# A feed-forward stage without GpSimd: leaky ReLU as one ScalarE activation, low parts on VectorE

## The chip, the cores and the metric

The kernel runs on one core of one Trainium2 chip. The metric is the device time of one execution in microseconds, the median of several runs. TensorE multiplies matrices (weights are loaded by a separate step, PEld), VectorE and ScalarE work elementwise here on SBUF and PSUM, GpSimd elementwise on SBUF, and SyncE (SP) issues the DMAs.

## The reference

A block of three parts. The first is a linear attention with a complex decay over batch 4, 8 heads, 768 positions and head size 48. The second is a soft mixture of 8 experts with 4 slots each. The third, the one that the change touches, is a feed-forward on 3072 tokens of width 384 with a hidden width of 2048:

```
h = x @ w_in                  # [3072, 384] @ [384, 2048]
g = np.maximum(0.01 * h, h)   # leaky ReLU, slope 0.01
return g @ w_out              # [3072, 2048] @ [2048, 384]
```

`x` is the output of the mixture, `c @ slot_out`, with `c` the softmax of the logits over 32 slots. Its rank is therefore 32, and the kernel multiplies `slot_out @ w_in` first (`product`), which leaves an inner dimension of 32 for `h`.

## The kernel before

**Number format.** Matmuls of the feed-forward take fp32r operands. To keep accuracy a value is split in two: the high part is the value written as fp32r, the low part is the value minus the high part, also written as fp32r. An output tile adds three products: high by high, low by high, high by low.

**Tiling.** The 3072 tokens form 8 groups (j = 0 to 7) of 384 tokens, and the hidden width forms 16 blocks (f) of 128. For one pair (j, f) `ffn1` (lines 1004 to 1016) has one matmul of 128x384 into a PSUM bank (line 1007). Line 1009 (ScalarE) copies 0.01 times the bank to an SBUF tile `x`, line 1010 (VectorE) takes the maximum of this tile and the bank, line 1011 (ScalarE) writes the high part into a tile of tag `w`, and the low part is made by GpSimd for j = 1 (line 1013) and by VectorE for all other j (line 1015). `ffn2` (lines 1020 to 1038) then has three matmuls for each of the three token tiles of j (lines 1028 to 1030); a bank for each tile adds up over all 16 f. After the last f line 1037 copies the bank out and line 1038 stores it.

**Output weights.** `w_out` arrives as 64-bit words, one block of 384 columns for each f. `conv_wo` loads a block into one of two `raw` buffers, and `narrow` (lines 417 to 424) makes fp32 of it in five steps: line 420 on ScalarE, lines 421, 422, 423 and 424 on VectorE, through one of two `tmp` buffers. Then GpSimd writes the high part (line 452) and the low part (line 453). `conv_wi` uses the same `narrow` for the input weights, much earlier and without the split.

**Loops.** Groups j = 0 and 1 run together, f by f: for each f a conversion four blocks ahead, two `ffn1` two blocks ahead and six `ffn2` steps, 20 matmuls in all. This needs six output banks, and leaves two of the eight for `ffn1`. Groups j = 2 to 7 follow one by one, when all weights are split.

**Order.** Nothing is issued in source order. Every operation is put into a planner with its engine, an estimated cost (`c_dve`, `c_act`, `c_ptt`, `c_pts`), its operands and its results; the planner goes backward from the end to give each a latest time, and forward to write an order for each engine. Every engine then works through its own list in order. Costs of moved operations thus enter the order of the whole program. The activation tables of ScalarE are loaded where the planner says (line 251).

Of the kernel before, what the change touches and what calls it, by code (L numbers as in the profile page):

```python
# [10 lines left out]
F32 = mybir.dt.float32  # L11
F32R = mybir.dt.float32r
I32 = mybir.dt.int32
AF = mybir.ActivationFunctionType
ALU = mybir.AluOpType
# [15 lines left out]
NG = 3 * P  # L31
# [240 lines left out]
def c_dve(n):  # L272
    return 0.069 + 1.04e-3 * n
# [6 lines left out]
def c_act(n):  # L280
    return 0.095 + 0.83e-3 * n


def c_ptt(n):
    return 0.15 + 2.11e-3 * n


def c_pts(n):
    return 0.1 + 0.92e-3 * n
# [3 lines left out]
def tile_kernel(  # L293
# [14 lines left out]
    V, A, GP, T, SY = nc.vector, nc.scalar, nc.gpsimd, nc.tensor, nc.sync  # L308
# [3 lines left out]
    def pe(cost, fn, r=(), w=(), **k):  # L312
        return plan.add("PE", cost, fn, r, w, **k)

    def act(n, fn, r=(), w=(), **k):
        return plan.add("ACT", c_act(n), fn, r, w, **k)

    def dve(cost, fn, r=(), w=(), **k):
        return plan.add("DVE", cost, fn, r, w, **k)

    def pool(cost, fn, r=(), w=(), **k):
        return plan.add("POOL", cost, fn, r, w, **k)
# [29 lines left out]
    HW = W // 2  # L352
# [75 lines left out]
    def conv(src, i, dst):  # L428

        raw = t_raw()  # L430
        load(raw, None, src[:, 2 * HW * i:2 * HW * (i + 1)].rearrange("p (n w) -> p n w", w=2), P * HW * 8)
        tmp = t_tmp()
        d, dk = dst(tmp)
        narrow(
            HW, d, dk, raw, lambda: raw()[:, :, 0], lambda: raw()[:, :, 1],
            (tmp, 0), (tmp, 1), lambda: tmp()[:, 0], lambda: tmp()[:, 1],
        )
        return tmp
# [7 lines left out]
    def conv_wo(i):  # L446
        j, h = divmod(i, 2)
        if h == 0:
            woh[j], wol[j] = t_w([P, 2, HW], F32R), t_w([P, 2, HW], F32R)
        tmp = conv(wo_in, i, lambda tmp: (lambda: tmp()[:, 1], (tmp, 1)))  # L450
        wh, wl = woh[j], wol[j]
        pool(c_pts(HW), lambda: GP.tensor_scalar(wh()[:, h], tmp()[:, 1], 1.0, 0.0, op0=ALU.mult, op1=ALU.add), [(tmp, 1)], [(wh, h)])
        pool(c_ptt(HW), lambda: GP.tensor_tensor(wl()[:, h], tmp()[:, 1], wh()[:, h].bitcast(F32), op=ALU.subtract), [(tmp, 1), (wh, h)], [(wl, h)])


    st = [dict() for _ in range(NU)]
# [547 lines left out]
    def ffn1(j, f):  # L1004
        b = bank()
        w, o = gs[f // 4], P * (f % 4)
        pe(0.17, lambda: T.matmul(b()[:, :NG], lhsT=w()[:, o:o + P], rhs=cT[j](), start=True, stop=True), [(w, o // 256), cT[j]], [b])  # L1007
        u, g = t_x(), t_w([P, 2, NG], F32R)
        act(NG, lambda: A.activation(u(), b()[:, :NG], AF.Copy, scale=0.01), [b], [u])  # L1009
        dve(c_dve(NG), lambda: V.tensor_tensor(u(), u(), b()[:, :NG], op=ALU.max), [b], [u])  # L1010
        act(NG, lambda: A.activation(g()[:, 0], u(), AF.Copy), [u], [(g, 0)])  # L1011
        if j == 1:
            pool(c_ptt(NG), lambda: GP.tensor_tensor(g()[:, 1], u(), g()[:, 0].bitcast(F32), op=ALU.subtract), [u, (g, 0)], [(g, 1)])
        else:
            dve(c_dve(NG), lambda: V.tensor_tensor(g()[:, 1], u(), g()[:, 0].bitcast(F32), op=ALU.subtract), [u, (g, 0)], [(g, 1)])  # L1015
        hl[j, f] = g

    ob = {}
# [38 lines left out]
    for f in FO[:4]:  # L1057
        conv_wo(f)
    for f in FO[:ahead]:
        for j in range(2):  # L1060
            ffn1(j, f)
    for i, f in enumerate(FO):
        if i < NFC - 4:
            conv_wo(FO[i + 4])
        for j in range(2):
            if i + ahead < NFC:
                ffn1(j, FO[i + ahead])
        for j in range(2):
            for t in range(3):
                ffn2(j, t, f)  # L1070
    for j in range(2, NB):
        if j == 3:
            combine_t(6, NB, bank, ("cw", 6))
        for f in FO:
            ffn1(j, f)
            if j < NB - 1:
                for t in range(3):
                    ffn2(j, t, f)
# [54 lines left out]
```

## Time and profile before

| | |
|---|---|
| median of 3 runs | 546.22 us (546.16 to 546.89) |
| profiled execution | 546.49 us, span 544.8 us |
| mean granted TensorE clock | 0.997 |
| busy: TensorE matmul | 492.4 us (90%) |
| busy: VectorE | 401.4 us (74%) |
| busy: ScalarE | 367.0 us (67%) |
| busy: GpSimd | 56.9 us (10%), 75 instructions |

The busy shares are means over stages that differ. The page divides the span into 40 slices of 13.6 us, and the stage of the feed-forward begins in slice 23, counted from 1. A group of the profile is all instructions of one line, engine and shape; "idle before" is the time that the engine stood still just before them, with what ended it. In a timeline consecutive instructions of one group can be merged (x2, x3).

### The profile page before, as it was taken

The page shows a single profiled execution, that of the slowest core. Times are in us where ns is not written, and L with a number is a line of the kernel's source. Part 1 is how long each engine was busy: PE and PEld are TensorE (multiplying, and loading weights), DVE is VectorE, ACT ScalarE, POOL GpSimd, SP SyncE. Part 2 cuts the span into 40 slices and gives each one's busy share as a digit, 9 for nine tenths or more (in the row PEclk, how much of TensorE's full clock was granted, in tenths as well). Part 3 has the DMA queues.
Part 4 walks back from the last instruction along what each step waited for, and adds up shares of the span by engine and source line. Part 5 has one row for each costly group of instructions (what it writes and reads, how often), then busy time and mean ns, then how long its engine had stood idle before and what let it go on. Part 6 is the DMA issues. An engine that isn't in the chain of part 4 may idle for free.

```text
span 544.8 us, 10467 instructions
## 1 busy us (share of the span) xinstructions
PE 492.4 (90%) x3985; PEld 432.5 (79%) x3985; DVE 401.4 (74%) x796; ACT 367.0 (67%) x693; POOL 56.9 (10%) x75
## 2 busy tenths in 40 slices
PE   2488979999999999997898877779999999999997
PEld 1277768888889888885544766779999999999997
DVE  2577898998999999897525999986548643986510
ACT  7879999799999986945103644547457545976612
POOL 1000000000000000001002566660000000000000
PEclk9999999999999999999899999999999999999999
DMA  7953254442353586878794233311010002000002
GB/s 273 393 155 109 42 147 143 131 143 80 88 170 78 168 265 225 292 259 255 254 403 135 60 87 88 87 31 43 1 58 16 2 1 73 29 1 2 29 1 101
DMA packets 43846, 66.98 MB, mean 123 GB/s; under 512 B 19098, under 2 KB 24970, under 8 KB 43796
## 3 DMA queue, kind: packets, MB, share of 16 engines
q1 hardware_dynamic: 43476, 66.29, 37.5%
q8 instruction: 31, 0.51, 0.4%
q0 software_dynamic: 320, 0.03, 0.1%
q14 instruction: 19, 0.16, 0.1%
HBM read 61.53 MB, written 4.75 MB: 122 GB/s over the span
## 4 chain that ended last, share of the span: by engine, by line
PE 60%; DVE 18%; ACT 11%; DMA 7%; issue 3%; SPq 0%; ACTq 0%; DVEq 0%
PE b L1029 10%; PE b L1030 10%; PE b L1028 10%; PE btr L622 6%; PE bm L662 5%; PE bsc L637 5%; PE bm L680 4%; PE bc L545 4%; PE b L1007 3%; DMA w<-in_w_dram 3%; DVE tmp L421 3%; ACT L251 2%; DVE tmp L423 2%; DVE tmp L422 2%; DVE x L1010 2%
## 5 line engine op out<-in xcount | busy, mean ns | idle before, releaser
L1028 PE MATMUL b<-w 128*128 128x384 f32 x384 | 129.0, 336 | 0.7 <-ACT w L1011 0.6
L1029 PE MATMUL b<-w 128*128 128x384 f32 x384 | 129.0, 336 | 0.5 <-DVE w L1015 0.5
L1030 PE MATMUL b<-w 128*128 128x384 f32 x384 | 128.5, 335 | 0.0
L1010 DVE TENSOR_TENSOR x<-x,b 128x384 f32<-128x384 f32 x128 | 68.9, 550 | 40.1 <-ACT x L1009 38.6
L1011 ACT ACTIVATE w<-x 128x384 fp32r<-128x384 f32 x128 | 65.6, 525 | 43.9 <-DVE x L1010 39.2
L1015 DVE TENSOR_TENSOR w<-x,w 128x384 fp32r<-128x384 f32 x112 | 62.0, 566 | 15.7 <-PE b L1007 8.9
L1028 PEld LDWEIGHTS b<-w 128*128 128x128 f32 x384 | 72.1, 188 | 1.6 <-issue 0.9
L1029 PEld LDWEIGHTS b<-w 128*128 128x128 f32 x384 | 72.1, 188 | 1.0 <-DVE w L1015 1.0
L1009 ACT ACTIVATE x<-b 128x384 f32<-128x384 f32 x128 | 60.3, 487 | 18.6 <-PE b L1007 8.6
L1030 PEld LDWEIGHTS b<-w 128*128 128x128 f32 x384 | 72.1, 188 | 0.0
L637 PE MATMUL bsc<-qt,kt 96*128 96x128 f32 x384 | 51.7, 280 | 0.1
L637 PEld LDWEIGHTS bsc<-qt,kt 96*128 96x128 f32 x384 | 46.6, 193 | 2.6 <-issue 1.5
L640 DVE TENSOR_TENSOR sc<-bsc,tri_r 128x512 f32<-128x512 f32 x48 | 32.8, 685 | 12.8 <-PE bsc L637 9.1
L1037 ACT ACTIVATE k<-b 128x384 f32<-128x384 f32 x24 | 11.8, 492 | 43.2 <-PE b L1030 42.8
L662 PE MATMUL bm<-sc,w 128*64 128x128 f32 (+1 forms) x384 | 37.7, 282 | 2.0 <-ACT x L711 1.3
L1007 PE MATMUL b<-q,qt 128*128 128x384 f32 x80 | 26.5, 356 | 13.5 <-DVE x L1010 13.4
L622 PE MATMUL btr<-ident,q 128*96 128x128 f32 x192 | 30.6, 283 | 5.4 <-DVE q L607 5.0
L251 ACT ACT_TABLE_LOAD x27 | 34.6, 1283 | 1.2 <-PEq L1122 0.8
L680 PEld LDWEIGHTS bm<-w,k 128*96 128x96 f32 x320 | 31.7, 170 | 4.6 <-ACT x L711 2.3
L680 PE MATMUL bm<-w,k 128*96 128x48 f32 x320 | 33.6, 252 | 1.9 <-ACT x L711 1.9
L628 ACT ACTIVATE qt<-btr 96x512 f32<-96x512 f32 x48 | 28.0, 589 | 7.0 <-PE btr L622 4.5
L662 PE MATMUL bm<-qt,S 96*48 96x128 f32 x320 | 31.2, 272 | 0.0
(175 smaller groups left out, 862.3 us busy)
## 6 DMA issues: line engine op xcount, KB each, us to landing
w<-in_w_dram SPq DMA_DIRECT2D x49, 384.0 KB, 5.7
w<-in_qkv_dram SPq DMA_DIRECT2D x36, 384.0 KB, 4.2
w<-in_a_dram SPq DMA_DIRECT2D x22, 384.0 KB, 4.6
raw<-in_wi_dram SPq DMA_DIRECT2D x16, 384.0 KB, 3.5
raw<-in_wo_dram SPq DMA_DIRECT2D x16, 384.0 KB, 3.2
out_dram<-k SPq DMA_DIRECT2D x24, 192.0 KB, 1.9
cs<-in_w_dram SPq DMA_DIRECT2D x6, 384.0 KB, 5.8
k<-in_w_dram SPq DMA_DIRECT2D x6, 192.0 KB, 5.1
```

What stands on the lines that cost most here:

```text
L251: self.preload(TABLES[o.table])
L622: T.transpose(b()[:96, P * i:P * i + P], src()[:, i].rearrange("p t d -> p (t d)"), ident)
L637: T.matmul(b()[:, P * i:P * i + P], lhsT=k()[:96, i, :], rhs=q()[:96, i, :], start=True, stop=True)
L662: T.matmul(y()[64 * j:64 * j + m, o:o + P], lhsT=l, rhs=r, start=kind == 0, stop=kind == 1 or c == 0)
L680: T.matmul(b()[:96, o:o + n], lhsT=k()[:, i].rearrange("p t d -> p (t d)"), rhs=v()[:, D * g:D * g + n], start=True, stop=True)
L1009: act(NG, lambda: A.activation(u(), b()[:, :NG], AF.Copy, scale=0.01), [b], [u])
L1010: dve(c_dve(NG), lambda: V.tensor_tensor(u(), u(), b()[:, :NG], op=ALU.max), [b], [u])
L1011: act(NG, lambda: A.activation(g()[:, 0], u(), AF.Copy), [u], [(g, 0)])
L1015: dve(c_dve(NG), lambda: V.tensor_tensor(g()[:, 1], u(), g()[:, 0].bitcast(F32), op=ALU.subtract), [u, (g, 0)], [(g, 1)])
L1028: T.matmul(b()[:, :DM], lhsT=lh, rhs=wh()[:, i], start=f == FO[0], stop=False)
L1029: T.matmul(b()[:, :DM], lhsT=ll, rhs=wh()[:, i], start=False, stop=False)
L1030: T.matmul(b()[:, :DM], lhsT=lh, rhs=wl()[:, i], start=False, stop=f == FO[-1])
```

## The change

Two functions change. In `conv_wo` the high part of the output weights is written by ScalarE and the low part by VectorE. In `ffn1` one ScalarE activation, Prelu with alpha 0.01, takes the place of the scaled copy and the maximum, and the low part is on VectorE for every j. GpSimd keeps a copy in `combine_t` (line 853).

```diff
@@ conv_wo
-        pool(c_pts(HW), lambda: GP.tensor_scalar(wh()[:, h], tmp()[:, 1], 1.0, 0.0, op0=ALU.mult, op1=ALU.add), [(tmp, 1)], [(wh, h)])
-        pool(c_ptt(HW), lambda: GP.tensor_tensor(wl()[:, h], tmp()[:, 1], wh()[:, h].bitcast(F32), op=ALU.subtract), [(tmp, 1), (wh, h)], [(wl, h)])
+        act(HW, lambda: A.activation(wh()[:, h], tmp()[:, 1], AF.Copy), [(tmp, 1)], [(wh, h)])
+        dve(c_dve(HW), lambda: V.tensor_tensor(wl()[:, h], tmp()[:, 1], wh()[:, h].bitcast(F32), op=ALU.subtract), [(tmp, 1), (wh, h)], [(wl, h)])
@@ ffn1
-        act(NG, lambda: A.activation(u(), b()[:, :NG], AF.Copy, scale=0.01), [b], [u])
-        dve(c_dve(NG), lambda: V.tensor_tensor(u(), u(), b()[:, :NG], op=ALU.max), [b], [u])
+        act(NG, lambda: A.activation(u(), b()[:, :NG], AF.Prelu, alpha=0.01), [b], [u])
         act(NG, lambda: A.activation(g()[:, 0], u(), AF.Copy), [u], [(g, 0)])
-        if j == 1:
-            pool(c_ptt(NG), lambda: GP.tensor_tensor(g()[:, 1], u(), g()[:, 0].bitcast(F32), op=ALU.subtract), [u, (g, 0)], [(g, 1)])
-        else:
-            dve(c_dve(NG), lambda: V.tensor_tensor(g()[:, 1], u(), g()[:, 0].bitcast(F32), op=ALU.subtract), [u, (g, 0)], [(g, 1)])
+        dve(c_dve(NG), lambda: V.tensor_tensor(g()[:, 1], u(), g()[:, 0].bitcast(F32), op=ALU.subtract), [u, (g, 0)], [(g, 1)])
```

## Rows read from the trace of the kernel before

**Rows 1.** The page: busy tenths of 40 equal slices of the span.
```profile
PE   2488979999999999997898877779999999999997
...
DVE  2577898998999999897525999986548643986510
...
POOL 1000000000000000001002566660000000000000
```

**Rows 2.** Windows: length, then per engine busy us (instructions); clock, DMA.
```profile
299.92:365.45 65.53, 51.43 (x268) 45.87 (x269) 64.84 (x104) 34.42 (x76) 39.49 (x42) 1.00 0.26 73
386.00:413.50 27.50, 27.50 (x161) 27.46 (x161) 14.06 (x29) 15.80 (x37) 0.00 (x0) 1.00 0.10 37
```

**Rows 3.** Timeline of TensorE: start us, length us, engine, line, [idle before].
```profile
341.00 0.44 PE L1007 MATMUL b<-q,qt 128*128 128x384 f32 x1 [1.49 <-DVE x L1010]
...
345.78 0.44 PE L1007 MATMUL b<-q,qt 128*128 128x384 f32 x1 [1.02 <-DVE x L1010]
...
533.52 0.33 PE L1029 MATMUL b<-w 128*128 128x384 f32 x1
...
536.64 0.33 PE L1029 MATMUL b<-w 128*128 128x384 f32 x1
```

**Rows 4.** Timeline of VectorE, 340 to 346 us.
```profile
341.33 0.55 DVE L1010 TENSOR_TENSOR x<-x,b 128x384 f32<-128x384 f32 x1
341.80 0.68 DVE L1015 TENSOR_TENSOR w<-x,w 128x384 fp32r<-128x384 f32 x1
342.41 1.17 DVE L421 TENSOR_SCALAR tmp<-tmp 128x384 f32<-128x384 f32 x1
343.61 1.05 DVE L422 TENSOR_SCALAR tmp<-tmp 128x384 int32<-128x384 int32 x1
344.69 0.56 DVE L423 SCALAR_TENSOR_TENSOR tmp<-raw,tmp 128x384 int32<-128x384 int32 x1
345.17 0.55 DVE L1010 TENSOR_TENSOR x<-x,b 128x384 f32<-128x384 f32 x1
```

**Rows 5.** Groups, VectorE, 325 to 361 us: busy us, mean ns | idle before.
```profile
L421 DVE TENSOR_SCALAR tmp<-tmp 128x384 f32<-128x384 f32 x7 | 8.2, 1169 | 0.0
```

**Rows 6.** Groups, 20 to 280 us, three engines.
```profile
L421 DVE TENSOR_SCALAR tmp<-tmp 128x384 f32<-128x384 f32 x16 | 5.5, 354 | 2.4 <-ACT tmp L420 2.3
...
L853 POOL TENSOR_SCALAR kt<-logits 128x192 fp32r<-128x192 f32 x8 | 3.2, 404 | 71.1 <-PE bsc L637 38.1 <-PE b L920 24.0 <-DVE sc L640 4.9
...
L569 ACT ACTIVATE cs<-cs,b_hpi 128x384 f32<-128x384 f32 x1 | 0.6, 603 | 0.0
```

**Rows 7.** One line's instructions: the table loads, min/median/max ns.
```profile
L251 ACT ACT_TABLE_LOAD  x27: 1283/1283/1283, 0.8 to 226.0; - x27
```

**Rows 8.** Timeline, 290 to 300 us, the start of the stage.
```profile
290.92 0.36 DVE L421 TENSOR_SCALAR tmp<-tmp 128x384 f32<-128x384 f32 x1 [4.65 <-ACT tmp L420]
...
291.32 0.36 DVE L422 TENSOR_SCALAR tmp<-tmp 128x384 int32<-128x384 int32 x1
...
293.93 1.26 DVE L423 SCALAR_TENSOR_TENSOR tmp<-raw,tmp 128x384 int32<-128x384 int32 x1
...
299.92 0.41 PE L1028 MATMUL b<-w 128*128 128x384 f32 x1 [0.60 <-ACT w L1011]
```

**Rows 9.** Timeline of ScalarE, 340 to 346 us.
```profile
340.98 0.53 ACT L1011 ACTIVATE w<-x 128x384 fp32r<-128x384 f32 x1 [2.44 <-DVE x L1010]
341.41 0.54 ACT L420 ACTIVATE tmp<-raw 128x384 f32<-128x384 f32 x1
341.92 0.53 ACT L1011 ACTIVATE w<-x 128x384 fp32r<-128x384 f32 x1
342.35 0.92 ACT L1009 ACTIVATE x<-b 128x384 f32<-128x384 f32 x2
```

**Rows 10.** Tile raw, 290 to 372 us: issue to landing of its loads.
```profile
DMA to landing us min/median/max: 3.0/3.2/3.4
```

**Rows 11.** Groups, 290 to 365 us: the weight copies on GpSimd.
```profile
L452 POOL TENSOR_SCALAR w<-tmp 128x384 fp32r<-128x384 f32 x15 | 7.8, 518 | 36.8 <-DVE tmp L424 27.0 <-PE b L1007 9.8
```

## The prediction

> **What bounds the kernel now.** I read the page first. Its slices tell two stages of the feed-forward apart: in slices 23 to 27 (counted from 1) VectorE stands at 8 or 9, TensorE at 7 or 8 and GpSimd at 5 or 6; from slice 28 on TensorE stands at 9 and GpSimd at 0 [rows 1]. Then I cut the stage with the windows view, from the first output matmul (299.92) to the place where the chain of waits goes over to TensorE (365.45). There VectorE is busy 64.84 of 65.53 us, GpSimd 39.49, ScalarE only 34.42, and TensorE shows 268 matmuls; afterwards TensorE is busy all of the time (27.50 of 27.50) and VectorE half of it; the granted clock is 1.00 in both, the higher of its two levels, 2.4 GHz [rows 2]. In the later stretch matmuls of this shape start 0.1733 us apart: 18 of them between 533.52 and 536.64 [rows 3]. So the 268 needed 46.4 us, and TensorE lost 65.5 - 46.4 = 19.1 us in the first stretch. Everything behind it is a full TensorE, so a microsecond won there reaches the end whole. That loss is the most that the stage can give back.
>
> The period shows who makes it. The first of the two matmuls of line 1007 starts at 341.00 and, one f later, at 345.78, and each time it waited for the maximum of line 1010 on VectorE, which holds its PSUM bank [rows 3]. One step of f costs 4.78 us in which TensorE has 2 + 18 = 20 matmuls, 20 x 0.1733 = 3.47 us. The timeline of VectorE shows where 4.78 comes from: seven instructions, and two of them, the scalar operations of lines 421 and 422, take 1.17 and 1.05 us, while GpSimd computes [rows 4]. Over 325 to 361 us line 421 averages 1169 ns [rows 5]. The same line, same shape, converts the input weights between 20 and 280 us, where GpSimd does little (eight copies of 404 ns), and takes 354 ns, 16 times over [rows 6]; line 422 does the same. The two lose some 0.8 and 0.7 us to their neighbour.
>
> **The change part by part.** *Counts.* For one f (both j of 0 and 1), VectorE loses two maxima (line 1010) and gains the low part of j = 1 and the low part of the weights: seven instructions before and seven after. Moved work alone wins nothing there; the gain must come from what each instruction costs once GpSimd is silent. GpSimd keeps only the copy of line 853, eight of them, all before 280 us [rows 6], so the stage has none left.
>
> *VectorE after.* The two scalar operations fall to 0.36 us, and since each waits for the one ahead of it, some 0.40 apart (290.92 to 291.32 when the first weights are converted [rows 8]). The other five start 0.47 us apart where nothing holds them: 345.17 - 344.69 = 0.48, 341.80 - 341.33 = 0.47 [rows 4]. Sum: 0.40 + 0.40 + 5 x 0.47 = 3.15 us. The low part of the weights has no row on VectorE; its nearest rows are lines 1015 and 1010 of the same shape, at 0.47 apart (0.55 of record) and, beside GpSimd, 0.61 apart (0.68) [rows 4]. I take 0.47, since no GpSimd is beside it; 0.61 would make the sum 3.3.
>
> The Trainium skill, "VectorE: DVE Perf Modes", section "The DRAIN you can't avoid", says that the pipe is flushed behind each operation and that the next one waits, though one that is not held starts earlier. The trace bears the exception: starts 0.47 us apart under records of 0.55. Without the exception the sum would be that of the records, 2 x 0.36 + 5 x 0.55 = 3.47, a tie with TensorE.
>
> *ScalarE after.* For one f it has the two copies of line 1009, two of line 1011 and line 420 now; the first two become Prelu, and one weight copy is added. Starts lie 0.43 apart (340.98 to 341.41) and 0.51 behind line 420 (341.41 to 341.92) [rows 9]: 5 x 0.43 + 0.51 = 2.66 us. No row shows a Prelu. Nearest below is line 1009 itself, the copy that it takes the place of (0.49 each: 0.92 for two), nearest above an activation with a bias tensor at 603 ns [rows 6, 9]. I take 0.49, the same operands and shape. At 603 the sum is 2.9, still under 3.47, so both ends give one answer; below a copy nothing suggests it could go.
>
> The Trainium skill, "ScalarE: Activation LUTs", section "Table sets: the hidden batching unit", lists relu, copy, identity and abs as members of every set and does not name a parametric one. By it one load might be due before the first Prelu; a load takes 1283 ns here [rows 7], so the sum would be at most 1.3 us longer.
>
> *GpSimd.* Its 16 weight copies, 16 weight low parts and 16 low parts of j = 1 go. They were not on the path themselves.
>
> *What is late next.* TensorE with 3.47 against 3.15 and 2.66. Two things keep it from running without a gap. First, VectorE is at 91% with queues in order; an instruction that waits for its operand holds those behind it. Second, the loads of the output weights have two buffers: a buffer is free again after line 424, the load lands 3.2 us later [rows 10], then come line 420 (0.54) and 0.40 + 0.40 + 0.48 + 0.47 + 0.55 of VectorE, 6.04 us for two, 3.02 per f. That fits under 3.47 by 0.45. Issue of the loads on SP stays as it is. Line 453's place is taken by VectorE and frees the temporary earlier or at the same time. The bank of line 1007 is now free after one ScalarE activation and no longer after VectorE's maximum, which takes away the very wait that set the period.
>
> For these gaps I charge 2.5 us over the 16 f: little in steady state, most in the first 10 us, where VectorE has the last of the small product and three conversions at once. Bounds: 0 (everything hidden), and 7, if each of 16 f loses 0.45 more (3.9 in place of 3.47).
>
> *Start of the stage.* The first output matmul waits for line 1011 [rows 8], which waits for the maximum [rows 9]. A maximum (0.55) falls out of that chain. Earlier, line 423 took 1.26 us at 293.93 beside GpSimd, 0.7 over its later record of 0.56 [rows 4, 8]; against it stand the weight low parts, 0.47 each, now in VectorE's queue at that time. I take 0.6 us, between 0 and 1.4.
>
> *Later groups, j of 2 and above.* VectorE loses 16 maxima in each and ScalarE keeps its two activations; TensorE is full there already [rows 2], so nothing changes.
>
> **Sum:** -19.1 - 0.6 + 2.5 = -17.2 us. The profiled execution took 546.49 us (1.7 around its span of 544.8); its forecast is 529.3. The median of the runs shown is 546.22, 0.27 less, and the forecast for it is 529.0. Bounds of the terms: 546.2 - 19.1 - 1.4 = 525.7, and 546.2 - 19.1 + 7 = 534.1.
>
> **Rivals.**
> *The weight conversion is late.* VectorE in order and two load buffers make the conversions the bound. For it: 6.04 us for two loads holds only if ScalarE takes line 420 at once and VectorE nothing else in between; with three activations ahead of it (1.3) and two foreign VectorE instructions (0.94) it is 8.3, 4.15 per f. Counted from the third conversion at some 301 us (an estimate from the start of the stage), the 16th ends at 301 + 13 x 4.15 = 355, 3.7 us after TensorE would want it (299.3 + 15 x 3.47 = 351.4), beside the gaps of the forecast: 529.0 + 3.7 = 533, up to 537 with the start as it was. Against it: four conversions run ahead, and TensorE has slack to give.
>
> *Lines 421 and 422 stay slow.* Then VectorE needs 1.20 + 1.08 + 5 x 0.47 = 4.63 in place of 4.78, some 0.1 over about ten f: 545. Against it: 354 ns wherever GpSimd is idle [rows 6].
>
> *ScalarE is held by the weight copy (slower).* GpSimd stood idle 36.8 us ahead of 15 copies of line 452, mostly for line 424 [rows 11]; that was free. On ScalarE the same wait at the head of the queue holds the Prelus behind it, and so the banks, and line 1007. At 36.8 / 15 = 2.45 us per f ScalarE's period is 2.66 + 2.45 = 5.11, 0.33 over today's 4.78: 16 x 0.33 = 5.3, 551.5 us. It decides from 4.78 - 2.66 = 2.1 us of waiting per f; under 0.8 it costs nothing. For it: ScalarE also has line 420 of the same chain, which waits for a load. Against it: GpSimd was early because it had nothing else; on ScalarE the two Prelus and two copies of the f lie between, 1.7 us of the 2.45, and line 424 comes sooner once VectorE runs at 3.15.
>
> *Prelu and copy need different tables.* Then two loads of 1.28 for each of 128 Prelus: ScalarE 128 x (0.86 + 2.57) = 439 us against 241 of the stage, 744 us. Against it: the Abs of line 420 and the copies alternate behind the last load, which is at 226.0 us, and cost none [rows 7, 9]; the copy seems to come with any table.
>
> **How the numbers follow.** Forecast 0.68, its own range 525.7 to 534; conversion late 0.20 (533 to 537); slow scalar operations 0.06 (545; I count a third as no change, since a difference of 0.2%, 1.1 us, is about what a measurement can tell from none); ScalarE held 0.05; tables 0.01. Faster 0.68 + 0.20 + 0.04 = 0.92, same 0.02, slower 0.06. The range 526 to 536.5 leaves out the last three cases (0.12) and small parts of the first two.
>
> **What would show it.** In the changed profile lines 421 and 422 are at 0.36 us throughout; GpSimd has no work after 280 us; VectorE in the first 60 us of the stage falls from 99% to about 90%; line 1007 no longer waits for VectorE; TensorE stands at 9 from slice 23 on; the first outputs leave some 17 us earlier and the stage behind them is as long as before. If lines 421 and 422 are short and TensorE still idles over 5 us, the conversion chain or ScalarE's queue is the wait and the size is wrong; if they stay over 1 us, the reading is wrong.

## The result and the profile after

The changed kernel took 526.11 us in the median of four runs (524.99 to 529.43), the kernel before 546.56 us beside it: a ratio of 0.9623, 95% interval 0.9567 to 0.968. On the 546.22 us that the prediction started from, that is 525.6 us. The prediction said 529.0, with a range from 526.0, so the gain was 20.6 us where 17.2 were forecast. A second set of six runs (below) gave 0.9661, interval 0.9625 to 0.9696.

The page after, the slices that answer to [rows 1]. A slice is 13.1 us here; the feed-forward begins in slice 23.

```profile
PE   2478979999999999999799899999999999999997
...
DVE  2487699899899989988842799945430353025400
...
POOL 1000000000000000000000000000000000000000
```

TensorE, which stood at 7 or 8 in slices 23 to 27, now stands at 8 in slice 23, the first of the stage, and at 9 from there until the last slice; GpSimd is at 0. The windows view of the stage, which answers to [rows 2]: columns are the length, then busy us and instructions of TensorE, its weight loads, VectorE, ScalarE and GpSimd, then the granted clock.

```profile
310.00:330.00 20.00, 20.00 (x117) 20.00 (x117) 19.35 (x45) 18.94 (x46) 0.00 (x0) 1.00 0.42 119
330.00:350.00 20.00, 20.00 (x117) 20.00 (x116) 15.97 (x36) 9.11 (x19) 0.00 (x0) 1.00 0.29 80
```

VectorE is still nearly full (19.35 of 20.00 us), but it makes 45 instructions in that time, and TensorE is busy for all of both windows. The groups from 290 to 360 us, which answer to [rows 5] and [rows 11], show the price of each instruction. The change moves line numbers: line 1009 is now the Prelu, 1010 the high part on ScalarE, 1011 the low part on VectorE, 452 and 453 the weight parts on ScalarE and VectorE, and 1024 to 1026 the output matmuls.

```profile
L1011 DVE TENSOR_TENSOR w<-x,w 128x384 fp32r<-128x384 f32 x39 | 20.7, 553 | 10.1 <-ACT w L1010 9.3 <-PE b L1007 0.8
...
L1009 ACT ACTIVATE x<-b 128x384 f32<-128x384 f32 x41 | 18.5, 489 | 1.4 <-PE b L1007 1.3
...
L423 DVE SCALAR_TENSOR_TENSOR tmp<-raw,tmp 128x384 int32<-128x384 int32 x16 | 8.9, 556 | 0.4
...
L453 DVE TENSOR_TENSOR w<-tmp,w 128x384 fp32r<-128x384 f32 x16 | 8.9, 553 | 0.8 <-ACT w L452 0.8
L452 ACT ACTIVATE w<-tmp 128x384 fp32r<-128x384 f32 x16 | 8.4, 523 | 6.1 <-DVE tmp L424 6.1
...
L422 DVE TENSOR_SCALAR tmp<-tmp 128x384 int32<-128x384 int32 x16 | 5.8, 360 | 0.5
...
L421 DVE TENSOR_SCALAR tmp<-tmp 128x384 f32<-128x384 f32 x16 | 5.7, 355 | 2.5 <-ACT tmp L420 2.5
```

Line 421 fell from 1169 to 355 ns; line 1009, now the Prelu, takes the 489 ns that were assumed; the weight copy on ScalarE waited 6.1 us for line 424 over 16 f, 0.4 per f, and in the two windows above TensorE lost nothing by it. The number of table loads is still 27, the last at 226.2 us: Prelu needed none.

**Where the 20.6 us came from.** Three points of TensorE's timeline split the span: the first matmul of the small product (line 982), the first output matmul and the last one. Before:

```profile
292.64 2.80 PE L982 MATMUL b<-wi,so 128*32 128x256 f32 x48 [0.53 <-DVE so L964]
...
296.18 0.38 PE L991 MATMUL b<-w,sc 128*128 128x256 f32 x1 [0.43 <-DVE w L986]
...
297.11 0.72 PE L1007 MATMUL b<-q,qt 128*128 128x384 f32 x3
...
540.97 0.34 PE L1030 MATMUL b<-w 128*128 128x384 f32 x1
```

with the first output matmul at 299.92 [rows 8]. After:

```profile
292.39 2.80 PE L982 MATMUL b<-wi,so 128*32 128x256 f32 x48 [0.49 <-DVE so L964]
...
295.34 0.28 PE L991 MATMUL b<-w,sc 128*128 128x256 f32 x1
...
296.16 0.73 PE L1007 MATMUL b<-q,qt 128*128 128x384 f32 x3
...
298.19 0.34 PE L1024 MATMUL b<-w 128*128 128x384 f32 x1
298.81 0.44 PE L1025 MATMUL b<-w 128*128 128x384 f32 x1 [0.28 <-DVE w L1011]
...
520.40 0.34 PE L1026 MATMUL b<-w 128*128 128x384 f32 x1
```

| part | before | after | difference |
|---|---|---|---|
| ahead of the product (start of line 982) | 292.64 | 292.39 | -0.25 |
| start: line 982 to the first output matmul | 7.28 | 5.80 | -1.48 |
| stage: first to last output matmul | 241.05 | 222.21 | -18.84 |

The third row is the measure that I use below for the experiments, from one profiled execution of each. Executions of one kernel differ by some 5 us in the total, but not in the stage: the second profile of the changed kernel had its last table load at 229.8 us instead of 226.2, and its stage took 222.25 us. Behind the last output matmul the two spans are equal to 0.1 us.

### The profile page after: what moved, and what is told of

It is laid out like the page before. It is cut to its first block, busy times and chain, and to the rows that moved or that the text cites. A ratio compares the mean times of both kernels' runs of the same rounds, so it can differ in the third digit from the quotient of the medians.

```text
span 524.1 us, 10310 instructions
## 1 busy us (share of the span) xinstructions
PE 488.1 (93%) x3985; PEld 433.3 (83%) x3985; DVE 333.8 (64%) x700; ACT 367.3 (70%) x709; POOL 12.8 (2%) x27
## 4 chain that ended last, share of the span: by engine, by line
PE 80%; ACT 12%; DVE 4%; DMA 2%; issue 1%; SPq 0%; ACTq 0%; DVEq 0%
PE b L1025 13%; PE b L1026 13%; PE b L1024 13%; PE bm L662 7%; PE btr L622 7%; PE bsc L637 6%; PE bm L680 4%; PE bc L545 4%; PE b L1007 4%; PE b L909 3%; ACT L251 3%; PE b L945 2%; PE bm L707 1%; PE bm L750 1%; ACT kt L628 1%
## 5 line engine op out<-in xcount | busy, mean ns | idle before, releaser
L1011 DVE TENSOR_TENSOR w<-x,w 128x384 fp32r<-128x384 f32 x128 | 68.2, 556 | 100.8 <-ACT w L1010 97.8
L1010 ACT ACTIVATE w<-x 128x384 fp32r<-128x384 f32 x128 | 63.4, 527 | 11.3 <-PE b L1026 9.7
L1009 ACT ACTIVATE x<-b 128x384 f32<-128x384 f32 x128 | 58.4, 489 | 9.3 <-DVE w L1011 4.4
L622 PE MATMUL btr<-ident,k 128*96 128x128 f32 x192 | 29.4, 279 | 1.4 <-ACT kt L628 1.1
L622 PEld LDWEIGHTS btr<-ident,q 128*96 128x96 f32 x192 | 21.0, 133 | 10.4 <-DVE q L607 5.7
```

Source lines behind the costliest of these rows:

```text
L622: T.transpose(b()[:96, P * i:P * i + P], src()[:, i].rearrange("p t d -> p (t d)"), ident)
L1009: act(NG, lambda: A.activation(u(), b()[:, :NG], AF.Prelu, alpha=0.01), [b], [u])
```

## Experiments

My theory was the prediction's: VectorE bounds the first stretch because GpSimd, working beside it, holds its instructions; take GpSimd away, and TensorE is the bound. The rival: the number of VectorE instructions is what counts. The summary first; "stage" is first to last output matmul in us, and "VectorE" the number of its wanted instructions per f. The experiments were timed in three groups, and the kernel before took 546.85 (1 to 4), 546.39 (5 to 8) and 548.80 us (9 to 12) beside them, so rows are compared by the stage or the ratio. Line numbers shift by a few from run to run; the text names the lines that moved.

| run | VectorE | GpSimd per f | stage | median us | ratio (95%) |
|---|---|---|---|---|---|
| before | 7 | 3 | 241.1 | 546.2 | 1 |
| after | 7 | 0 | 222.2 | 526.1 | 0.9623 (0.9567 to 0.968) |
| no Prelu, no GpSimd | 9 | 0 | 229.1 | 534.4 | 0.977 (0.9708 to 0.9832) |
| Prelu only | 5 | 3 | 239.8 | 544.0 | 0.9945 (0.9917 to 0.9974) |
| after, idle two-input work on GpSimd | 7 | 2 | 236.5 | 540.2 | 0.9862 (0.9827 to 0.9896) |
| after, idle one-input work on GpSimd | 7 | 4 | 230.7 | 534.8 | 0.9765 (0.9718 to 0.9813) |
| after, weight low part twice | 8 | 0 | 224.3 | 527.5 | 0.9609 (0.9577 to 0.964) |
| after, three times | 9 | 0 | 228.8 | 534.3 | 0.9739 (0.969 to 0.9789) |
| weights moved only | 8 | 1 | 231.0 | 537.9 | 0.9801 (0.9748 to 0.9855) |
| after, j = 1 on GpSimd | 6 | 1 | 230.0 | 535.3 | 0.9762 (0.9718 to 0.9806) |

**1. The change without Prelu.**

```diff
-        act(NG, lambda: A.activation(u(), b()[:, :NG], AF.Prelu, alpha=0.01), [b], [u])
+        act(NG, lambda: A.activation(u(), b()[:, :NG], AF.Copy, scale=0.01), [b], [u])
+        dve(c_dve(NG), lambda: V.tensor_tensor(u(), u(), b()[:, :NG], op=ALU.max), [b], [u])
```

> The changed kernel with the scaled copy and the maximum back in place of Prelu; no work for GpSimd in the stage. VectorE has nine instructions per f, two more than before the change. Theory (GpSimd's neighbourhood is what cost the time): 2 x 0.40 + 7 x 0.47 = 4.09 us per f, 0.62 over TensorE's 3.47; the stage of 13.7 such periods loses some 8.5 us against the changed kernel, and the maximum in the starting chain 0.8: about 535.5 us, still 2% faster than before, with lines 421 and 422 at 0.36 us. Rival (the number of VectorE instructions is what cost the time): nine in place of seven, 13.7 x 2 x 0.47 = 13 us slower than before, 559 us.

Measured: 534.4 us, stage 229.1, lines 421 and 422 at 346 ns. The groups over 298 to 365 us:

```profile
L422 DVE TENSOR_SCALAR tmp<-tmp 128x384 int32<-128x384 int32 x14 | 4.8, 346 | 0.0
L421 DVE TENSOR_SCALAR tmp<-tmp 128x384 f32<-128x384 f32 x14 | 4.8, 346 | 0.0
```

Two more VectorE instructions per f than before, and 12 us less. The rival by count falls. This profile has a stretch at a lower clock: TensorE waited 1.11 and 0.76 us at its first output matmuls, then ran ten matmuls 0.32 us apart (granted clock 0.83 over 300 to 310 us, 1.2 GHz in the stretch), about 1.5 us more than at the higher level. How much of that reaches the end isn't shown, so the 229.1 may be up to 1.5 too long as a price of the nine instructions.

**2. Prelu alone, on the kernel before.**

```diff
-        act(NG, lambda: A.activation(u(), b()[:, :NG], AF.Copy, scale=0.01), [b], [u])
-        dve(c_dve(NG), lambda: V.tensor_tensor(u(), u(), b()[:, :NG], op=ALU.max), [b], [u])
+        act(NG, lambda: A.activation(u(), b()[:, :NG], AF.Prelu, alpha=0.01), [b], [u])
```

> The kernel before with Prelu alone; GpSimd keeps the weights and j = 1. VectorE has five instructions per f. Theory: lines 421 and 422 still meet GpSimd, 1.20 + 1.08 + 0.48 + 0.47 + 0.61 = 3.84 us per f, 0.37 over TensorE: 5 us over the changed kernel and 0.9 at the start, 532 us. Rival (the count of instructions): 2 x 0.40 + 3 x 0.47 = 2.2 us, TensorE bound, 526 to 527 us.

Measured: 544.0 us, stage 239.8. Both forecasts miss: with two VectorE instructions fewer per f almost nothing is won. The timelines of VectorE and GpSimd show why (start us, length us; line 1014 is VectorE's low part, 1012 GpSimd's):

```profile
334.76 1.25 DVE L423 SCALAR_TENSOR_TENSOR tmp<-raw,tmp 128x384 int32<-128x384 int32 x1
336.05 0.56 DVE L424 SCALAR_TENSOR_TENSOR tmp<-raw,tmp 128x384 int32<-128x384 int32 x1
336.53 1.33 DVE L1014 TENSOR_TENSOR w<-x,w 128x384 fp32r<-128x384 f32 x2
337.78 1.18 DVE L421 TENSOR_SCALAR tmp<-tmp 128x384 f32<-128x384 f32 x1
338.99 1.05 DVE L422 TENSOR_SCALAR tmp<-tmp 128x384 int32<-128x384 int32 x1
340.07 1.24 DVE L423 SCALAR_TENSOR_TENSOR tmp<-raw,tmp 128x384 int32<-128x384 int32 x1
```

```profile
337.42 1.31 POOL L1012 TENSOR_TENSOR w<-x,w 128x384 fp32r<-128x384 f32 x1
338.70 1.12 POOL L453 TENSOR_TENSOR w<-tmp,w 128x384 fp32r<-128x384 f32 x1
339.78 1.11 POOL L1012 TENSOR_TENSOR w<-x,w 128x384 fp32r<-128x384 f32 x1
```

Three VectorE instructions in a row end soon after a GpSimd one ends (338.96 after 338.73, 340.04 after 339.82, 341.31 after 340.89): by these rows the two engines take turns. And line 423, with two SBUF inputs, is held like the scalar ones; I had counted it as free. Before, the maxima stood in that place, and they read PSUM and were not held (0.55 us each in [rows 4]). Prelu took away the two instructions that GpSimd didn't slow. In this run's waits over 300 to 372 us ScalarE also stood 15.0 us, 9 times, for loads of the output weights, since line 424, which frees the buffer, came late; and TensorE ran some 3.5 us at a granted clock below full (0.83 in 350 to 360 us) behind a longer wait, matmuls 0.32 us apart, the lower level of 1.2 GHz, which costs this profile about 1.6 us of its 239.8.

**3 and 4. Work on GpSimd that nobody reads, on the changed kernel.** The most direct test: nothing waits for it.

```diff
+        for _ in range(2):
+            pool(c_ptt(HW), lambda: GP.tensor_tensor(acc, wh()[:, h].bitcast(F32), wl()[:, h].bitcast(F32), op=ALU.subtract), [(wh, h), (wl, h)], ['acc'])
```

and in run 4

```diff
+        for _ in range(4):
+            pool(c_pts(HW), lambda: GP.tensor_scalar(acc, wl()[:, h].bitcast(F32), 1.0, 0.0, op0=ALU.mult, op1=ALU.add), [(wl, h)], ['acc'])
```

> The changed kernel with two subtractions of 128x384 per f on GpSimd whose result nobody reads (high part minus low part of the output weights, into a tile that is free by then). Nothing waits for them. Theory (GpSimd's two-input work holds VectorE's scalar operations): lines 421 and 422 rise from 0.36 to about 1 us wherever they fall beside one, VectorE 4.0 to 4.65 us per f, 533 to 543 us. Rival (no contention; GpSimd cost only as a step of the chain): 526 us and 0.36 us.

> The same with four single-input scalar operations per f on GpSimd (0.51 us each, the same busy time as two subtractions). Theory A (any GpSimd instruction holds them until it ends): at most 0.5 us for each of lines 421 and 422, 3.6 to 4.1 us per f, 528 to 535 us. Theory B (only its two-input instructions do): 526 us, 0.36 us.

Measured: 540.2 and 534.8 us, stages 236.5 and 230.7. Idle GpSimd work costs 14.3 and 8.5 us of stage; so contention alone makes up most of the 18.8 that the change won there, and theory A holds for the single-input kind. The groups of VectorE over 298 to 365 us, first with the two-input work, then with the one-input work (line 1013 is the low part on VectorE, 455 the idle work):

```profile
L1013 DVE TENSOR_TENSOR w<-x,w 128x384 fp32r<-128x384 f32 x33 | 23.7, 743 | 0.4 <-ACT w L1012 0.4
...
L423 DVE SCALAR_TENSOR_TENSOR tmp<-raw,tmp 128x384 int32<-128x384 int32 x14 | 12.1, 865 | 0.3
...
L421 DVE TENSOR_SCALAR tmp<-tmp 128x384 f32<-128x384 f32 x14 | 6.5, 466 | 0.0
```

```profile
L455 POOL TENSOR_SCALAR acc<-w 128x384 f32<-128x384 f32 x58 | 36.3, 626 | 26.7 <-DVE w L453 22.9
...
L1013 DVE TENSOR_TENSOR w<-x,w 128x384 fp32r<-128x384 f32 x37 | 25.4, 709 | 5.7 <-ACT w L1012 5.7
...
L423 DVE SCALAR_TENSOR_TENSOR tmp<-raw,tmp 128x384 int32<-128x384 int32 x14 | 9.9, 710 | 0.3
...
L421 DVE TENSOR_SCALAR tmp<-tmp 128x384 f32<-128x384 f32 x14 | 5.5, 392 | 0.0
```

The expectation named lines 421 and 422; in fact instructions with two SBUF inputs are held too (1.37 us for one of line 423), and how much a line suffers is a matter of when it comes. The one-input work held them as well (line 423 at 710 ns, against 556). In both runs VectorE is busy 9.7 to 9.9 of every 10 us from 308 to 348, so it sets the stage there.

**5. The changed kernel again**, without an edit.

> The changed kernel itself, beside the others of this call: 526 us, ratio to before 0.962. The forecast was 529.0; if the ratio stays near 0.962 the miss of some 3 us is real and not the spread of four runs (524.99 to 529.43).

Measured: 529.15 us in the median of six, 525.64 to 530.2, ratio 0.9661; the stage 222.25. The forecast's 0.968 lies within this interval, so by the total alone the miss would be hard to tell. By the stage it is clear: 222.2 in both profiles, where the forecast's terms make 241.05 - 19.1 + 2.5 = 224.5.

**6 and 7. One and two more subtractions per f on VectorE that nobody reads** (in run 7 twice).

```diff
+        for _ in range(1):
+            dve(c_dve(HW), lambda: V.tensor_tensor(acc, wh()[:, h].bitcast(F32), wl()[:, h].bitcast(F32), op=ALU.subtract), [(wh, h), (wl, h)], ['acc'])
```

> The changed kernel with one more subtraction per f on VectorE, whose result nobody reads. VectorE then needs 3.15 + 0.47 = 3.62 us per f, 0.15 over TensorE. Theory (the conversions run some four f ahead, so VectorE's queue costs nothing until its sum outruns that lead): 16 x 0.15 = 2.4 us, which the lead hides: 526 to 527 us. Rival (the forecast's charge for queues in order, 2.5 us, plus the excess of 2.1): 530 to 531 us.

> Two of them: nine instructions per f, 4.09 us, 0.62 over TensorE, as many as with the maximum back, but none of the two is in the chain of ffn1. Theory: 16 x 0.62 = 9.9 us less a lead of about 4 us: 532 us. Rival (charge for the queues plus the whole excess): 526 + 8.5 + 2.5 = 537 us.

Measured: 525.9 and 526.3 us, no cost for either, against the 532 of the second expectation. The test was flawed: the planner put the instructions where VectorE has time. The group in the run with two, from 298 to 350 us and from there to 520:

```profile
L455 DVE TENSOR_TENSOR acc<-w 128x384 f32<-128x384 f32 x8 | 4.4, 549 | 0.0
```

```profile
L455 DVE TENSOR_TENSOR acc<-w 128x384 f32<-128x384 f32 x23 | 12.7, 554 | 0.3
```

Work that nothing waits for says nothing on a queue; it has to be work that is wanted.

**8. The product and the first four `ffn1` ahead of the conversions.** A try at a version that beats both.

```diff
+    plan.lead = 8.0
     product()
+    plan.lead = 0.0
...
+    plan.lead = 8.0
     for f in FO[:ahead]:
         for j in range(2):
             ffn1(j, f)
+    plan.lead = 0.0
```

> The changed kernel with the small product and the first four ffn1 given priority over the conversions in the planner (lead 8 us), nothing else. In the changed profile a weight copy on ScalarE (296.41) stands ahead of the first Prelu (296.82) and a weight low part on VectorE (296.96) ahead of the last casts of the product; the first output matmul starts at 298.19 and the second waits 0.28 us for the low part. Theory: 0.4 to 0.6 us sooner at the start, and the end with it: 525.5 us. Rival (the conversions that are put back are then late for the third f): no gain or a loss, 526 to 527 us.

Measured: 525.83 us, ratio 0.963 (0.9594 to 0.9665), not to be told from the changed kernel. Line 982 to the first output matmul took 5.84 us against 5.80, the stage 222.6: the instructions that I put back were not what the first matmul waited for. In both traces TensorE has no gap from line 982 to the first output matmul, so nothing could be won ahead of it. The 0.28 us wait behind it is gone here, but at 328 us line 420 waits 1.13 us for its load, the Prelus behind it are late, and TensorE loses 0.8 us there: the rival's mechanism, late conversions.

**9 and 10. The weight low part computed twice and three times**, wanted work this time.

```diff
+        for _ in range(2):
+            dve(c_dve(HW), lambda: V.tensor_tensor(wl()[:, h], tmp()[:, 1], wh()[:, h].bitcast(F32), op=ALU.subtract), [(tmp, 1), (wh, h)], [(wl, h)])
-        dve(c_dve(HW), lambda: V.tensor_tensor(wl()[:, h], tmp()[:, 1], wh()[:, h].bitcast(F32), op=ALU.subtract), [(tmp, 1), (wh, h)], [(wl, h)])
```

> The changed kernel with the low part of the output weights computed twice on VectorE, the second over the first, so that the extra instruction is one that the matmuls wait for and can't be put off. VectorE 3.62 us per f, 0.15 over TensorE's 3.47. I read the stage from the first to the last output matmul, 222.2 us in the changed kernel whatever its start. Theory (work ahead hides queues): 13.7 x 0.15 = 2.1 us at most, less the lead of some 4 us with which the conversions end: 222 to 224 us. Rival (the forecast's charge: 2.5 us for queues in order, beside the excess): 226 us or more.

> Three times: nine instructions per f that are all wanted, 4.09 us. Theory (once the lead is used up VectorE's sum sets the stage): 13.7 x 0.62 = 8.5 us less up to 4: 227 to 231 us, near the 229.1 of the kernel without Prelu, which has as many instructions, so a total of 531 to 535. Rival (the lead hides this too, as the idle work of the run before was hidden): 223 us.

Measured: stages 224.3 and 228.8, that is 2.1 and 6.6 us over the changed kernel, where VectorE's excess over TensorE is 13.7 x 0.15 = 2.1 and 13.7 x 0.62 = 8.5 (13.7 is the first stretch in periods of before, 65.53 / 4.78). The first lies just above its theory's 222 to 224 and below the rival's 226, the second within its theory's range. At most the excess comes out, with nothing on top. The stage goes by the larger of the two sums, in experiment 10 by 1.9 us less than that; the forecast's 2.5 us for queues in order isn't there. Nine instructions per f give 228.8 us here and 229.1 in the kernel without Prelu, which has the slow stretch named above.

**11. Only the weights moved**, on the kernel before: the first part of the change alone.

```diff
-        pool(c_pts(HW), lambda: GP.tensor_scalar(wh()[:, h], tmp()[:, 1], 1.0, 0.0, op0=ALU.mult, op1=ALU.add), [(tmp, 1)], [(wh, h)])
-        pool(c_ptt(HW), lambda: GP.tensor_tensor(wl()[:, h], tmp()[:, 1], wh()[:, h].bitcast(F32), op=ALU.subtract), [(tmp, 1), (wh, h)], [(wl, h)])
+        act(HW, lambda: A.activation(wh()[:, h], tmp()[:, 1], AF.Copy), [(tmp, 1)], [(wh, h)])
+        dve(c_dve(HW), lambda: V.tensor_tensor(wl()[:, h], tmp()[:, 1], wh()[:, h].bitcast(F32), op=ALU.subtract), [(tmp, 1), (wh, h)], [(wl, h)])
```

> The kernel before with the output weights split by ScalarE and VectorE, and nothing else: scaled copy and maximum stay, j = 1 keeps its low part on GpSimd. VectorE eight instructions per f, two of them reading PSUM. Theory (GpSimd's remaining 1.1 us per f holds some VectorE instruction for about 0.75): 2 x 0.40 + 6 x 0.47 + 0.75 = 4.37 us, stage 222.2 + 13.7 x 0.90 = 234.5 us, total 538 us. Rival (only the weights' work on GpSimd did the harm): 3.62 us, stage 224, total 528 to 530.

Measured: stage 231.0, total 537.9, between the two. GpSimd's one remaining instruction per f (1.13 us) holds VectorE for less than the 0.75 that I took: (231.0 - 222.2) / 13.7 = 0.64 over TensorE's 3.47 makes 4.11 us per f, 0.49 over the 3.62 of eight instructions. The groups from 298 to 362 us:

```profile
L1010 DVE TENSOR_TENSOR x<-x,b 128x384 f32<-128x384 f32 x33 | 17.9, 543 | 0.5 <-ACT x L1009 0.5
...
L423 DVE SCALAR_TENSOR_TENSOR tmp<-raw,tmp 128x384 int32<-128x384 int32 x14 | 9.7, 692 | 0.0
```

The maximum, one input of which is in PSUM, stays at 543 ns over all 33; line 423 rises to 692.

**12. The change with j = 1 back on GpSimd.**

```diff
-        dve(c_dve(NG), lambda: V.tensor_tensor(g()[:, 1], u(), g()[:, 0].bitcast(F32), op=ALU.subtract), [u, (g, 0)], [(g, 1)])
+        if j == 1:
+            pool(c_ptt(NG), lambda: GP.tensor_tensor(g()[:, 1], u(), g()[:, 0].bitcast(F32), op=ALU.subtract), [u, (g, 0)], [(g, 1)])
+        else:
+            dve(c_dve(NG), lambda: V.tensor_tensor(g()[:, 1], u(), g()[:, 0].bitcast(F32), op=ALU.subtract), [u, (g, 0)], [(g, 1)])
```

> The changed kernel with the low part of j = 1 back on GpSimd. VectorE six instructions per f. Theory (a hold of 0.75 for 1.1 us of GpSimd): 2 x 0.40 + 4 x 0.47 + 0.75 = 3.43 us, about TensorE's 3.47: stage 222 to 224, total 526 to 528. Rival (with Prelu every VectorE instruction of the stage reads two SBUF inputs or is a scalar one, so each microsecond of GpSimd holds VectorE for more than one, as with Prelu alone): 4 us per f, stage 229, total 533.

Measured: stage 230.0, total 535.3. My theory (222 to 224) falls; the rival (229) fits in size. One instruction less for VectorE and one of 1.12 us for GpSimd cost 7.8 us. The sum of VectorE alone doesn't explain it: 0.80 + 4 x 0.47 + 0.82 = 3.5, TensorE's 3.47, where 0.82 is what the records of its lines over 298 to 360 us are longer per f than in the changed kernel; and VectorE is busy 46.6 of 50 us from 298 to 348, not all of it. The waits of 298 to 355 us (engine, line, for whom: us, times, longest) name the rest:

```profile
ACT w L452 <- DVE tmp L424: 14.9, 12, 2.4
PEld b L1007 <- ACT x L1009: 7.4, 14, 1.6
```

And one place, VectorE, then ScalarE, then TensorE:

```profile
316.72 1.25 DVE L424 SCALAR_TENSOR_TENSOR tmp<-raw,tmp 128x384 int32<-128x384 int32 x1
...
318.01 0.53 ACT L452 ACTIVATE w<-tmp 128x384 fp32r<-128x384 f32 x1 [1.65 <-DVE tmp L424]
...
318.87 0.86 ACT L1009 ACTIVATE x<-b 128x384 f32<-128x384 f32 x2
...
319.40 0.82 PE L1007 MATMUL b<-q,qt 128*128 128x384 f32 x2 [0.75 <-ACT x L1009]
```

GpSimd's low part runs from 316.44 to 317.56, and line 424 is held to 317.97; the weight copy waits for it at the head of ScalarE's queue, the Prelus behind it start later, and TensorE waits for them to free its banks. This is the rival "ScalarE is held by the weight copy" of the prediction; it comes to life when VectorE is held. It is read from the waits alone: no run moved that copy alone.

## Why the prediction was right, and where it was wrong

**The mechanism was right.** GpSimd's work held VectorE, VectorE held TensorE, and with GpSimd silent TensorE is the bound: lines 421 and 422 at 355 and 360 ns, GpSimd without work behind 280.6 us, line 1007 no longer waiting for VectorE, the stage at TensorE's own rate. The prediction said that GpSimd keeps only the copies of line 853; it also issues ten transfers (line 532), the last at 203.5 us, outside the stage. Experiments 1, 3 and 4 show the hold: 3 and 4 put GpSimd work back with all else in place, and 1 takes it away without Prelu. The "GPSIMD Engine Reference" of the Trainium skill, section "Key points", says that GpSimd shares SBUF interfaces with VectorE, and that instructions in a two-port mode or with two SBUF inputs contend. The runs agree with the half on two SBUF inputs: line 423 took 865 ns beside the idle two-input work and 556 alone, and the maximum with a PSUM input stayed at 543. Line 421 has one input and took 1169 ns beside GpSimd [rows 5] and 355 alone; no row tells the mode in which it ran, so the other half is neither borne out nor denied. I had read only the scalar operations off the profile before, since in steady state line 423 happened to stand where GpSimd was idle; the 1.26 us of one of its instructions in [rows 8] was the hint.

**The step that failed: "For these gaps I charge 2.5 us over the 16 f".** The range began at 526.0, above the 525.7 that the bounds of the terms gave, and 525.6 lies just below both. Between the first and the last output matmul there are 1273 starts; at 0.1733 they take 220.6 us, and two groups of three transposes (line 858) add 0.7, 0.33 each in the chain of waits. TensorE therefore lost about 0.9 of 222.2 us, not 2.5, and half of that at one place: the second output matmul, at 298.81, starts 0.62 behind the first where 0.17 would have done, with a wait of 0.28. Experiments 9 and 10 show the reason: the stage follows the larger of VectorE's and TensorE's sums, and an engine at 91% or even 97% whose instructions are ordered ahead of need costs no more.

**The start was too small: 0.6 taken, 1.48 measured**, beyond the upper bound of 1.4. From line 982 to line 991 it took 3.54 us before and 2.95 after, and 2.95 also without Prelu, but 3.53 with Prelu alone: 0.59 is GpSimd beside the product's VectorE work. From line 1007 to the first output matmul it took 2.81 and 2.03: 0.78 is the maximum with its two hand-overs, where I had put down its 0.55 alone and then set the new low parts against it. Those cost nothing there. With Prelu alone that second piece took 2.05, and without Prelu 3.30, so how much the maximum costs goes by the order of the queues too.

**The loss was a little larger than read.** By 220.6 + 0.7 the stage before lost 19.7 us; counting 268 records gave 19.1. With 0.25 ahead of the product, which no run explains, the terms close: 17.2 + 1.6 + 0.9 + 0.6 + 0.25 = 20.55 us.

**The rivals.** The conversions were not late: the last low part of the weights was done at 347.3 us, and TensorE wanted the 16th f at about 298.2 + 15 x 3.47 = 350.2. The scalar operations did not stay slow. No table was loaded. ScalarE was held for 0.4 us per f, under the point from which I said that it would cost; experiment 12 shows that it can.

**The parts don't add up.** Without GpSimd the stage falls by 11.9 us (241.1 to 229.1), with Prelu alone by 1.3, with both by 18.8. Prelu is worth 6.9 us once GpSimd is silent, or 5.4 if all of the slow stretch of experiment 1 counts, since only then does VectorE's sum go by the number of its instructions.

## What to carry to other kernels

GpSimd work is not free because nobody waits for it: price it by what it does to VectorE's instructions with two SBUF inputs, or scalar ones like line 421, and compare their times in a stretch where GpSimd is idle. Where two engines are near each other, sum each by start-to-start distances and take the larger; a charge for queues needs a wait in the profile that shows it. Moving an instruction between engines may be worth nothing until another one has gone, so try the parts together as well as alone.

## What the hardware showed that I had not expected

- VectorE and GpSimd take turns, instruction by instruction: 1.25 and 1.18 us for VectorE instructions of 0.56 and 0.36, each ending 0.2 to 0.4 us after the GpSimd one beside it. GpSimd pays too: its 0.51 us scalar operation averaged 626 ns in experiment 4 (511 at the least).
- A VectorE instruction with one input in PSUM was not held. Line 1010 over 325 to 361 us, before and in experiment 1, that is with GpSimd at work and without:

```profile
L1010 DVE TENSOR_TENSOR x<-x,b 128x384 f32<-128x384 f32 x16 | 8.8, 548 | 0.0
```

```profile
L1010 DVE TENSOR_TENSOR x<-x,b 128x384 f32<-128x384 f32 x18 | 9.7, 536 | 0.1
```

- Prelu with an immediate slope took the 489 ns of the copy, and no table load.
